# One adaLN transformer block: loads in a new order, idle products first, LN2 normalisation on ScalarE, a new order of instructions

## The chip, the core and the metric

The kernel runs on one core of a Trainium2 chip. Five engines work side by side, each through its own list of instructions, in order: TensorE (PE: matrix products; PEld: its weight loads), VectorE (DVE), ScalarE (ACT), GpSimd (POOL) and SyncE (SP), which issues the transfers (DMAs). Semaphores make one engine wait for another. The metric is the device time of one execution in microseconds (us). "Clock" is the mean granted TensorE clock, 1.00 being full speed. Each run is put down as fast or slow; slow means over 1.5% above the fastest run of the same kernel.

## The reference

An adaLN block on x (2048 x 512, bf16): six modulation vectors from c, sliding local attention with 8 dilated taps and 32 heads, and a SwiGLU FFN with F = 1792.

```python
mod = (_silu(c) @ w_mod).reshape(c.shape[0], 6, 1, -1)
sa, ca, ga, sb, cb, gb = (mod[:, i] for i in range(6))   # shortened
h = _layernorm(x, axis=-1) * (1 + ca) + sa               # LN1
x = x + ga * _A_ref(h, A_wqkv, A_wo)                     # local attention
h = _layernorm(x, axis=-1) * (1 + cb) + sb               # LN2
x = x + gb * _B_ref(h, B_w1, B_w3, B_w2)                 # SwiGLU FFN
```

## The kernel before

The program lists operations with their engine, cost and operands. A list scheduler turns them into one order for each engine, by a table of tuned priorities; semaphores follow from that order. The 2048 rows are 16 tiles T of 128. VectorE takes the statistics, GpSimd turns the variance into 1/sqrt(var + eps) with two 128x1 operations (an add, a power), and VectorE normalises:

```python
def ln_stats(which, T):                       # which: 0 for LN1, 1 for LN2
    i = which * NT + T
    ...
    o = p.op("dve", lambda e: e.bn_stats(st[:, i, :], x_sb[:, T, :]), ...)
    p.op("dve", lambda e: e.bn_aggr(mv[:, i, :], st[:, i, :]), ..., lead=o)
    o = p.op("pool", lambda e: e.tensor_tensor(rs[:, i, :], mv[:, i, 1:2], cst[:, 0:1], ALU.add), ...)
    p.op("pool", lambda e: e.tensor_tensor(rs[:, i, :], rs[:, i, :], cst[:, 1:2], ALU.pow), ..., lead=o)
    p.op("dve", lambda e: e.tensor_scalar(vn.at[:], x_sb[:, T, :], mv[:, i, 0:1], rs[:, i, :],
                                          op0=ALU.subtract, op1=ALU.mult), 350, ("nm", i), ...)
    return vn
```

The result xn is transposed on TensorE, four 128x128 blocks for each tile, and ScalarE applies scale and shift on the way out. The attention multiplies on VectorE: `pq` (128x4096, queries by shifted keys) and `vsh` (128x4096, weights by values), 16 of each, and TensorE sums them with small products. The attention gate is a product against a broadcast copy of silu(c):

```python
def gate(i):
    def mm(e):
        for t in range(KT):
            ins = e.matmul(bank(vm), csb[:, t, :], wm_g[i][:, t, :], start=(t == 0), stop=(t == KT - 1))
    p.op("pe", mm, 4 * MM, ...)
    p.op("act", lambda e: e.activation(dst[:], bank(vm), ACT.Copy), ...)
```

The softmax here doesn't subtract the row's maximum and nothing guards it: scores larger than these inputs give would overflow.

## Time and profile before

| | before |
|---|---|
| time, median of 3 runs | 255.11 us (255.0 to 255.56) |
| profiled span, clock | 253.2 us, 1.00 |
| first projection starts | 10.51 us |
| last VectorE attention product ends | 179.3 us |
| TensorE / VectorE / ScalarE / GpSimd busy | 239.0 / 191.7 / 111.4 / 32.0 us |

A page has the busy time of each engine, then the span in 40 slices, where a digit is a busy share in tenths (9 is 90% or more). A second view lists what an engine waited for: engine, waiting line, releaser, then total us, times and longest. A third, the timeline, gives start, length, engine, line, operation, output from inputs, and how many instructions the row holds.

### The profile page before, as it was taken

How to read it: one execution, taken by the hardware profiler on the slowest of the kernel's cores; microseconds unless marked ns; L12 is line 12 of the kernel's file. 1: busy time of each engine (PE TensorE's matmuls, PEld its weight loads, DVE VectorE, ACT ScalarE, POOL GpSimd, SP SyncE). 2: the span in 40 equal slices, each digit the busy share in tenths (PEclk: the TensorE clock that was granted, in tenths of full speed). 3: DMA queues.
4: the chain of work that ended last, by engine and by line, in shares of the span. 5: the costliest groups of instructions: out<-in, count | busy, mean ns of one | idle time of the engine just before them, and what ended most of it. 6: DMA issues, size and time to landing. Idle time of an engine off the chain costs nothing.

```text
span 253.2 us, 5473 instructions
## 1 busy us (share of the span) xinstructions
PE 239.0 (94%) x2262; PEld 140.4 (55%) x2296; DVE 191.7 (76%) x298; ACT 111.4 (44%) x198; POOL 32.0 (13%) x81
## 2 busy tenths in 40 slices
PE   0599989999999999999999999999999999999995
PEld 0367555655488666546654544556544444565562
DVE  4759889999998989999899899999952443432432
ACT  2159748864863347432462273334234322420120
POOL 6237641001000040000002200020030000000000
PEclk9999999999999999999999999999999999999999
DMA  6997999899954595322369145393001000000101
GB/s 193 359 324 189 293 350 331 210 331 284 241 123 140 142 310 196 64 31 62 106 194 295 54 104 85 87 310 103 4 0 44 0 0 21 21 3 21 41 23 41
DMA packets 45817, 36.29 MB, mean 143 GB/s; under 512 B 19408, under 2 KB 36576, under 8 KB 45792
## 3 DMA queue, kind: packets, MB, share of 16 engines
q1 hardware_dynamic: 45264, 35.94, 49.4%
q8 instruction: 18, 0.29, 0.5%
q10 hardware_dynamic: 528, 0.00, 0.1%
q14 instruction: 7, 0.06, 0.1%
HBM read 30.67 MB, written 5.26 MB: 142 GB/s over the span
## 4 chain that ended last, share of the span: by engine, by line
PE 87%; DVE 5%; DMA 2%; POOL 2%; issue 1%; SPq 0%; ACT 0%; DVEq 0%
PE pall L771 36%; PE pall L792 19%; PE pall L615 9%; PE pall L755 5%; PE pall L742 5%; PE pall L633 5%; PE pall L673 4%; PE pall L574 2%; DMA sb_x<-in_A_x_dram 2%; POOL sb_rs L555 1%; DVE sb_xn L558 1%; DVE sb_st L550 1%; POOL sb_rs L553 1%; DVE sb_pq L664 1%; DVE sb_hh L780 1%
## 5 line engine op out<-in xcount | busy, mean ns | idle before, releaser
L771 PE MATMUL pall<-sb_h,sb_w 128*128 128x512 bf16 (+1 forms) x548 | 100.0, 336 | 0.7
L771 PEld LDWEIGHTS pall<-sb_h,sb_w 128*128 128x128 bf16 x560 | 53.7, 97 | 41.4
L777 ACT ACTIVATE sb_sg<-pall 128x512 bf16<-128x512 f32 (+1 forms) x70 | 35.6, 511 | 70.6 <-PE pall L771 70.3
L780 DVE TENSOR_TENSOR sb_hh<-sb_sg,pall 128x512 bf16<-128x512 bf16 (+1 forms) x70 | 39.5, 577 | 26.0 <-PE pall L771 23.8
L792 PE MATMUL pall<-sb_w,sb_hh 128*128 128x512 bf16 x216 | 49.7, 379 | 0.4
L664 DVE TENSOR_TENSOR sb_pq<-sb_q,sb_kT 128x4096 bf16<-128x4096 bf16 x16 | 36.4, 2283 | 0.5 <-ACT sb_q L622 0.3
L792 PEld LDWEIGHTS pall<-sb_w,sb_hh 128*128 128x128 bf16 x224 | 21.4, 98 | 23.5 <-DVE sb_hh L780 0.2
L615 PE MATMUL pall<-sb_h,sb_wqkv 128*128 128x512 bf16 (+1 forms) x155 | 31.9, 344 | 0.3
L582 ACT ACTIVATE sb_h<-pall,sb_modc 128x512 bf16<-128x512 bf16 (+1 forms) x36 | 23.1, 708 | 18.7 <-PE pall L574 13.1
L553 POOL TENSOR_TENSOR sb_rs<-sb_mv,sb_cst 128x1 f32<-128x1 f32 x32 | 8.8, 276 | 151.4 <-DVE sb_mv L551 148.4
L733 DVE TENSOR_TENSOR sb_vsh<-sb_vsh,sb_al 128x4096 bf16<-128x4096 bf16 x12 | 27.3, 2285 | 0.4 <-DMA sb_vsh<-v_scratch_dram 0.4
L798 DVE TENSOR_TENSOR sb_o<-pall,sb_x 128x512 bf16<-128x512 f32 x16 | 11.0, 688 | 18.0 <-PE pall L792 18.0
L550 DVE BATCH_NORM_STATS2 sb_st<-sb_x 128x6 f32<-128x512 bf16 x32 | 21.8, 682 | 3.3 <-DMA sb_x<-in_A_x_dram 3.2
L555 POOL TENSOR_TENSOR sb_rs<-sb_rs,sb_cst 128x1 f32<-128x1 f32 x32 | 20.9, 654 | 2.5
L615 PEld LDWEIGHTS pall<-sb_h,sb_wqkv 128*128 128x128 bf16 x160 | 15.1, 101 | 11.0 <-ACT sb_h L582 0.7
L633 PE MATMUL pall<-sb_wqkv,sb_h 128*128 128x512 bf16 x63 | 17.6, 411 | 1.5 <-DVE sb_xn L558 1.3
L574 PE MATMUL pall<-sb_ident,sb_xn 128*128 128x128 bf16 x128 | 12.8, 227 | 6.4 <-DVE sb_xn L558 6.4
L673 PEld LDWEIGHTS pall<-sb_E,sb_pq 128*128 128x128 bf16 x512 | 14.7, 96 | 2.7 <-DVE sb_pq L664 0.6
L748 ACT ACTIVATE sb_ot<-pall 128x512 bf16<-128x512 f32 x16 | 9.6, 598 | 13.6 <-PE pall L742 13.6
L574 PEld LDWEIGHTS pall<-sb_ident,sb_xn 128*128 128x128 bf16 x128 | 9.5, 101 | 10.6 <-DVE sb_xn L558 6.9
L755 PE MATMUL pall<-sb_wo,sb_ot 128*128 128x512 bf16 x58 | 15.0, 379 | 0.3
L673 PE MATMUL pall<-sb_E,sb_pq 128*128 128x32 bf16 x512 | 15.1, 177 | 0.0
(59 smaller groups left out, 163.8 us busy)
## 6 DMA issues: line engine op xcount, KB each, us to landing
sb_vsh<-v_scratch_dram SPq DMA_DIRECT2D x48, 256.0 KB, 4.4
sb_vshx<-v_scratch_dram SPq DMA_DIRECT2D x16, 256.0 KB, 4.5
sb_wm_s<-in_w_mod_dram SPq DMA_DIRECT2D x2, 1024.0 KB, 6.6
v_scratch_dram<-sb_v SPq DMA_DIRECT2D x16, 128.0 KB, 5.0
sb_w<-in_B_w_dram SPq DMA_DIRECT2D x4, 512.0 KB, 7.9
out_dram<-sb_o SPq DMA_DIRECT2D x16, 128.0 KB, 1.7
sb_w<-in_B_w_dram SPq DMA_DIRECT2D x1, 1792.0 KB, 8.9
sb_wqkv<-in_A_wqkv_dram SPq DMA_DIRECT2D x3, 512.0 KB, 7.9
```

What stands on the lines that cost most here:

```text
L550: o = p.op("dve", lambda e: e.bn_stats(st[:, i, :], x_sb[:, T, :]), 670, k, r=[vx[T]], w=[vs])
L574: ins = e.transpose(b[:, col:col + P], vns[tt].at[:, ft * P:(ft + 1) * P], ident[:])
L615: ins = e.matmul(bank(vp)[:, 0:n], wqkv[:, t, col:col + P], vh.at[:, t, 0:n], start=(t == 0), stop=(t == KT - 1))
L633: ins = e.matmul(bank(vp), vh.at[:, t, tt * P:(tt + 1) * P], wqkv[:, t, 2 * D:3 * D], start=(t == 0), stop=(t == KT - 1))
L664: return e.tensor_tensor(vp.at[:], in0, in1, ALU.mult)
L673: ins = e.matmul(b[:, c0:c0 + H], vp.at[:, w, ft, :], E_sb[:, ft, :], start=(ft == 0), stop=(ft == KT - 1))
L733: return e.tensor_tensor(v_w, v_w, a_w, ALU.mult)
L755: ins = e.matmul(bank(vy), vt.at[:, ft, :], wo[:, ft, :], start=(ft == 0), stop=(ft == KT - 1))
L771: ins = e.matmul(bank(vp)[:, 0:n], wt[:, t, fi * P:(fi + 1) * P], vh.at[:, t, 0:n], start=(t == 0), stop=(t == KT - 1))
L777: p.op("act", lambda e: e.activation(vt.at[:, 0:n], bank(vgp)[:, 0:n], ACT.Silu), c_act(n), k, r=[vgp], w=[vt], table="silu")
L780: p.op("dve", lambda e: e.tensor_tensor(vh_.at[:, 0:n], vt.at[:, 0:n], bank(vup)[:, 0:n], ALU.mult), c_dve(n), k, r=[vt, vup], w=[vh_])
L792: ins = e.matmul(bank(vz), vhh[fi].at[:, tt * P:(tt + 1) * P], w2[:, fi, :], start=(fi == 0), stop=(fi == NF - 1))
```

## The change

The intent: keep TensorE warm from the start, take small work off it (gates, late transposes), take work off VectorE (the LN2 normalisation), load x of the first four tiles in pairs, and re-tune the order for this new list. All large loads were on SyncE's queue before and still are; what changes is their order, and the scheduler's estimate of when they land. c is now loaded in rows and transposed on TensorE. The core of the diff:

```diff
 def ln_stats(which, T):
     vn = Val("xn", xnpool)
+    if which:
+        vb = Val("nbias")
+        p.op("pool", lambda e: e.tensor_tensor(nb[:, T, :], mv[:, i, 0:1], cst[:, 2:3], ALU.mult), 200, ...)
+        p.op("pool", lambda e: e.tensor_tensor(nb[:, T, :], nb[:, T, :], rs[:, i, :], ALU.mult), 200, ...)
+        p.op("act", lambda e: e.activation(vn.at[:], x_sb[:, T, :], ACT.Identity, bias=nb[:, T, :],
+                                           scale=rs[:, i, :]), c_act(512) + 50, ("nm", i), ...)
+        return vn
     p.op("dve", lambda e: e.tensor_scalar(vn.at[:], ...), 350, ("nm", i), ...)
 ...
 def ln_T(which, gi, vns):
+    if which and gi >= DMA_T:                 # DMA_T = 3: tiles 10 to 15
+        for tt in range(n):
+            p.dma(lambda tt=tt: vh.at[:, :, tt * P:(tt + 1) * P], lambda tt=tt: vns[tt].at[:], ..., transpose=True)
+        ...                                   # scale and shift in place on ScalarE
 ...
+def warm(i, after=()):                        # four idle 128-column products
+    for _ in range(4):
+        ins = e.matmul(bank(vw)[:, 0:P], ones[:], ones[:], start=True, stop=True)
 ...
 def gate(i):
-    ins = e.matmul(bank(vm), csb[:, t, :], wm_g[i][:, t, :], ...)
+    ins = e.matmul(b[:, j:j + 1], wm_g[i][:, t, j * P:(j + 1) * P], csT_bf[:, t:t + 1], ...)
+    ...                                       # transpose, store to memory, load as a broadcast
 ...
+if T >= NT - 2:                               # last two tiles in halves of 256 columns
 ...
-for T in range(4):
-    p.dma(x_sb[:, T, :], x_view[:, T, :], ("load", 1 if T < 2 else 19), 131072, w=[vx[T]])
+p.dma(x_sb[:, 0:2, :], x_view[:, 0:2, :], ("load", 1), 262144, w=vx[0:2])
 ...
-    # table of priorities, all replaced by a new one
```

## The prediction

> **What bounds the kernel now.** I read the page first (busy shares and the 40 slices), then the waits of TensorE, the windows by stage, and the chain of waits with the timeline of the two ends. From the page of the kernel before:
>
> ```profile
> PE 239.0 (94%) x2262; PEld 140.4 (55%) x2296; DVE 191.7 (76%) x298; ACT 111.4 (44%) x198; POOL 32.0 (13%) x81
> ...
> PE   0599989999999999999999999999999999999995
> ...
> DVE  4759889999998989999899899999952443432432
> ...
> PEclk9999999999999999999999999999999999999999
> ```
>
> TensorE (PE) is full in nearly every slice; only the first two or three and the last have room. VectorE (DVE) is nearly as full, but only up to slice 28 (about 177 us). After that it has slack, and PE has not. PE's own waits are short and lie early:
>
> ```profile
> PE pall L574 <- DVE sb_xn L558: 6.4, 2, 5.6
> PE pall L522 <- DMA sb_wm_s<-in_w_mod_dram: 1.5, 1, 1.5
> PE pall L633 <- DVE sb_xn L558: 1.3, 1, 1.3
> PE pall L633 <- ACT sb_q L622: 0.2, 1, 0.2
> ```
>
> The columns are total us, times, longest. 9.4 us of waiting in all, nearly all before the first projection at 10.51 us. A busy share of 94% does not mean full speed, so I look at the spacing of products in the chain of waits (start, length, what):
>
> ```profile
> 10.51 3.59 PE pall L633 x8
> 14.10 0.85 PE pall L615 x4
> 14.95 0.21 PE pall L574 x2
> 15.16 0.85 PE pall L615 x4
> 16.02 0.21 PE pall L574 x2
> ...
> 22.24 0.45 PE pall L574 x8
> ...
> 37.84 0.79 PE pall L673 x32
> ...
> 80.82 3.49 PE pall L771 x32
> ...
> 87.49 0.86 PE pall L755 x4
> ...
> 250.34 0.69 DVE sb_o L798
> ```
>
> Warm rates follow: 0.86/4 = 216 ns for 512 columns, 3.49/32 = 109 ns for 256, 0.45/8 = 56 ns for a transpose, 0.79/32 = 25 ns for the small products. The first rows are slow: 3.59/8 = 449 ns for 512 columns, 0.85/4 = 212 ns for 256. That lasts until about 16 us. The granted-clock row says 9 tenths and more all along, so it does not show this slow start; only the spacing does.
>
> **Adding up the path.** Count of products times warm rate, from the first projection on: q and k 64 x 109 ns + 96 x 216 ns = 27.7 us; v 64 x 216 ns = 13.8; 120 transposes x 56 ns = 6.7; logits and value sums 2 x 512 x 25 ns = 25.3; output projection 13.8; FFN w1/w3 336 x 216 ns + 224 x 109 ns = 96.9; w2 224 x 216 ns = 48.3; second modulation 0.8; the two gates 8 x 216 ns = 1.7. Sum 235.0 us. The kernel takes from 10.51 to 250.3 us, 239.8 us. The difference is 4.8 us: 2.9 us of slow clock (below) and about 1.9 us of small stalls, of which the window from 22 to 40 us alone shows 1.0. Then comes a tail of 2.9 us to 253.2 (an add of 0.69 us, a store). Reported time is 1.9 us above the span (255.11 against 253.2).
>
> **What the Trainium skill says.** (1) "TensorE: Matmul & The Clock Gate", Part 1: the array starts at half clock and is released after about 3.4 us of sustained work. The trace agrees: 449 and 212 ns early, 216 and 109 ns from 16 us. (2) Same page, Part 3 and the gap table: small products cost about 25 ns however few columns. The trace has 25 ns. (3) "ScalarE: Activation LUTs", What ACT_TABLE_LOAD costs: 186 ns + 0.833 ns per column, plus about 93 ns for each per-partition operand, so 0.80 us for 512 columns with scale and bias. The trace's eviction of that form (L582) takes 781 ns. (4) "DMA: Bandwidth & Descriptors", DMA Transpose (X-bar): [...]two transposing streams must not overlap. All six here are on one queue. No run so far shows their duration.
>
> **The change, part by part.**
>
> *Idle products first.* 14 groups of four 128-column products on a tile of ones run from about 1.3 us, with 6 more groups after the first modulation. They fall into idle PE time and leave the array warm. Saved on the path: 8 x (449-216) + 4 x (212-109) x 2 + 4 x (105-56) ns = 1.86 + 0.82 + 0.20 = **2.9 us**. The first modulation (0.99 us cold, 0.78 us warm as at 39.51) is 0.2 us shorter, on the path to the first projection.
>
> *Gates as columns.* Each gate was 4 x 216 = 0.86 us on PE; now 16 one-column products x 25 ns + a small transpose, about 0.5 us. The vector goes to memory and returns as a broadcast, two chained transfers of some 2 to 3 us each (the small store and load of the attention weights take 2.5 us), long before wo is needed. Four VectorE instructions of 250 ns and two ScalarE copies of 0.6 us go. Saved on PE: **0.7 us**; a further 0.4 us if the first gate runs while PE waits for projections.
>
> *Transposes by DMA for T=10 to 15.* 24 x 56 ns = **1.3 us** leave PE. The DMAs are issued after 150 us, where the DMA share is low. They delay only h of the last two groups, while PE has earlier FFN work: hidden.
>
> *LN2 normalisation on ScalarE.* 16 x 0.40 = 6.4 us leave VectorE, 16 x 0.8 = 13 us come to ScalarE (44% busy). Neither is the bound; it only makes stalls rarer.
>
> *Last two tiles in halves.* Same PE time (28 x 109 against 14 x 216 ns), but the last add is of 256 columns (about 0.42 as against 0.69 us) and the last store half as large. Tail: **0.4 us** shorter.
>
> *c in rows.* Tanh waited for c until 3.74 us, while the modulation waited for its weights until 7.73: hidden.
>
> *New order of loads.* By the priorities: x2-3, x0-1, modulation weights, gate weights, x12-15, then v, q, wo, x8-11, k, x4-7. This is the cost. Before the v weights stand 0.52+1.05+0.52+0.52 MB, with them 3.1 MB. The windows show 0.96 MB by 5.6 us, then 365 GB/s to 10.5 (2.75 MB) and 349 GB/s after: 3.1 MB are there at about 11.6 us, as an estimate. Modulation and h would allow a start at about 10.3. The first projection thus slips from 10.5 to about 11.6: **1.1 us lost**, of which the first gate and group 1's eight transposes (0.4 + 0.4 us) fill most. K's weights come only at about 17.5 us, but v and q of T=0 to 3 (7 us) bridge that.
>
> **Sum.** -2.9 -0.7 -1.3 -0.4 +1.1 -0.8 = -5.0 us. For the new order I allow 0.7 us fewer small stalls, mainly those in 22 to 40 us: -5.7 us. 255.1 - 5.7 = **249.4 us**, 2.2% faster.
>
> **Rivals.** (a) *The first stage is bound by DMA.* With late weights the warm array waits instead, and the 2.9 us are lost to waits for wqkv. For it: DMA share 1.04 and 1.10 of 16 engines in 5.6 to 16 us. Against it: PE has other work once v has landed. It would cost up to 3 us: 252.5. (b) *VectorE is the hidden bound* up to 177 us: what PE saves it then waits for pq or attention sums. For it: VectorE is 93 to 98% busy from 40 to 180 us. Against it: it loses 6.4 us itself, and PE has FFN products to fill. About 251.5. (c) *The DMA transposes or the longer normalisation chain come late*, PE waits for h of the last groups, or SyncE's ordered queue holds up the attention loads. Against it: VectorE's attention ends near 177 us, and group [14, 15] is used only from about 220. About 251 to 253. (d) *The new order also removes the remaining stalls* and the first projection does not slip: the counts give 235.0 - 0.7 - 1.3 = 233.0, plus 10.3 start and 2.5 tail = 245.8 span, 247.7 us.
>
> **Range and chances.** The estimate lies almost on the 2% border (250.0 us). (d) sets the low side, (a) to (c) the high: 80% range 247.4 to 252.4 us. I give 0.57 to faster by over 2%, 0.41 to within 2%, and 0.02 to slower, since nothing adds work to PE outside its idle time.
>
> **What the profile after would show.** Products of 128 columns from about 1 us; the first v products 216 ns apart; else step one is wrong. First projection at 10.3 to 11.7 us; a wait of PE for wqkv over 1.5 us proves (a). 104 transposes on L574's successor plus three small ones, and gate products at 25 ns. PE's waits after 20 us under 1.5 us in all; over 3 us, named for VectorE, proves (b), for the transposing DMA or h after 150 us, (c). PE's last product near 245 us, the tail 2.5 us. Wrong would be a sum whose savings are seen yet return as stalls between 20 and 180 us.

## The result, and the profile after

| | before | after |
|---|---|---|
| time, median of 4 runs each, alternating | 255.06 us (254.55 to 255.56) | 268.5 us (264.67 to 270.22) |
| fast runs | all four | 267.99, 264.67 |
| profiled span, clock | 253.2 us, 1.00 | 268.4 us, 0.975 |
| first projection starts | 10.51 us | 15.03 us |
| last VectorE attention product ends | 179.3 us | 200.5 us |

The ratio is 1.0442 [95%: 1.0326, 1.0558]. A ratio here is the mean time of one kernel's fast runs over that of the other's fast runs of the same rounds, so it is not quite the ratio of the quoted medians. Where I turn a ratio into microseconds, I multiply its excess over 1 by 255.1: the changed kernel costs 11.3 us. Its profiled run is a slow one, at 270.22 us, but all four of its runs have a clock of 0.968 to 0.975, so the clock is no mark of the slow runs alone. The mean clocks of the two kernels are not quite comparable: that of the kernel before reads 1.00 from the start, although its first products are 449 ns apart (see the prediction), so its slow start is not in its mean.

The page of the changed kernel, same lines as those shown of before, with GpSimd's row added:

```profile
PE 246.7 (92%) x2376; PEld 149.2 (56%) x2407; DVE 187.0 (70%) x283; ACT 123.8 (46%) x214; POOL 54.1 (20%) x113
...
PE   7598999798579979699999999999999999999996
...
DVE  5568989799296896689999989882795344162342
...
POOL 5245122004240044600000450400462100000000
PEclk9889999999798999979999999999999999999999
```

TensorE has holes in slices 9 to 16 (counted from 0), some 60 to 114 us, where before it was full. GpSimd's busy time rose from 32.0 to 54.1 us for 32 more 128x1 operations. It is busy where TensorE has these holes, and again in slices 22 to 30, where TensorE stays full. TensorE's waits:

```profile
PE pall L629 <- ACT sb_xn L596: 9.1, 4, 3.4
PE pall L533 <- DMA sb_wm_s<-in_w_mod_dram: 2.5, 1, 2.5
```

The largest by far is for the normalised xn, from ScalarE. And ScalarE itself had waited for GpSimd:

```profile
ACT sb_xn L596 <- POOL sb_nb L595: 23.6, 11, 6.0
```

The timeline shows why. First the kernel before, one LN2 tile:

```profile
61.99 0.18 DVE L551 BATCH_NORM_AGGREGATE sb_mv<-sb_st 128x2 f32<-128x6 f32 x1
...
62.25 0.19 POOL L553 TENSOR_TENSOR sb_rs<-sb_mv,sb_cst 128x1 f32<-128x1 f32 x1 [21.04 <-DVE sb_mv L551]
...
62.52 0.55 POOL L555 TENSOR_TENSOR sb_rs<-sb_rs,sb_cst 128x1 f32<-128x1 f32 x1
...
62.88 0.39 DVE L703 TENSOR_TENSOR sb_tr<-sb_ex 128x256 f32<-128x256 f32 x1
...
65.09 0.73 DVE L558 TENSOR_SCALAR sb_xn<-sb_x,sb_mv,sb_rs 128x512 bf16<-128x512 bf16 x2
...
66.44 0.61 PE L574 MATMUL pall<-sb_ident,sb_xn 128*128 128x128 bf16 x8
```

The add takes 0.19 us and the power 0.55. Beside them VectorE runs short operations of the next tile and of the softmax. When it comes to the normalisation, rstd has long been there. Now the changed kernel, the first LN2 tile:

```profile
63.55 0.18 DVE L585 BATCH_NORM_AGGREGATE sb_mv<-sb_st 128x2 f32<-128x6 f32 x1
63.65 4.46 DVE L719 TENSOR_TENSOR sb_pq<-sb_q,sb_kT 128x4096 bf16<-128x4096 bf16 x2
...
63.81 2.14 POOL L587 TENSOR_TENSOR sb_rs<-sb_mv,sb_cst 128x1 f32<-128x1 f32 x1 [19.44 <-DVE sb_mv L585]
...
66.03 2.48 POOL L589 TENSOR_TENSOR sb_rs<-sb_rs,sb_cst 128x1 f32<-128x1 f32 x1
...
68.49 0.18 POOL L594 TENSOR_TENSOR sb_nb<-sb_mv,sb_cst 128x1 f32<-128x1 f32 x1
68.75 0.19 POOL L595 TENSOR_TENSOR sb_nb<-sb_nb,sb_rs 128x1 f32<-128x1 f32 x1
68.97 0.81 ACT L596 ACTIVATE sb_xn<-sb_x,sb_nb,sb_rs 128x512 bf16<-128x512 bf16 x1 [3.51 <-POOL sb_nb L595]
...
69.84 0.61 PE L629 MATMUL pall<-sb_ident,sb_xn 128*128 128x128 bf16 x4 [3.43 <-ACT sb_xn L596]
```

VectorE no longer normalises, so nothing keeps the scheduler from placing two `pq` products straight behind the statistics. They run from 63.65 to 68.11. The 0.19 us add takes 2.14 us and ends with the first product; the 0.55 us power takes 2.48 and ends 0.4 us after the second. The chain that took 0.8 us takes 5.1, and TensorE, whose transposes stand next in its order, waits 3.43 us. The profile has 11 GpSimd operations longer than 1.5 us after the change: one in LN1 and ten in LN2. Before it had two of that length and one of 1.42 us, all in LN1.

The Trainium skill states this case, on a page that the prediction did not use: "SBUF — State Buffer", Who interferes with whom. A VectorE instruction with both inputs in SBUF contends with a GpSimd instruction that reads SBUF, since they share a read interface, and the one that comes second waits until the first is done. The trace agrees: 2.14 and 2.48 us against 0.19 and 0.55, ending with the products.

The windows by stage say how much it costs (us from:to and length, busy us of PE, PEld, DVE, ACT and POOL, then clock, DMA share, GB/s). The changed kernel:

```profile
60.00:80.00 20.00, 14.45 (x251) 9.46 (x251) 15.07 (x20) 8.28 (x15) 8.22 (x8) 0.91 0.74 205
80.00:100.00 20.00, 19.24 (x249) 14.50 (x247) 16.40 (x21) 9.95 (x21) 3.20 (x4) 0.92 0.78 209
100.00:120.00 20.00, 16.64 (x175) 9.95 (x179) 14.29 (x18) 11.33 (x17) 6.97 (x13) 0.91 0.34 89
```

TensorE stands idle for 9.7 us here (5.55, 0.76 and 3.36), nearly all of it in four waits for xn of 3.43, 1.78, 1.56 and 2.29 us; in the kernel before it was 0.5 us in the same windows, at clock 1.00. The clock fell as well: 2 us slices show 0.50 in 70 to 72, in 80 to 82 and in 114 to 116 us, right behind the waits of 3.43, 1.78 and 2.29 us. A mean of 0.91 over 20 us means 3.6 us at half speed, which is 1.8 us of work lost; over the three windows 5.2 us. Together 14.9 us. This is a slow run, which lost 15.2 us of span in all. As a check the products done by a given time were counted by their weight loads, each product at its warm duration. The changed kernel is 3.3 us behind at 60 us (43.5 against 46.8 us of work) and 16.8 behind at 120 (90.0 against 106.8): 13.5 us are lost in those 60 us. From there to 180 us no more is lost, though GpSimd stands still four more times: by then TensorE has FFN products to go on with.

### The profile page after: what moved, and what is told of

It is laid out like the page before. It is cut to its first block, busy times and chain, and to the rows that moved or that the text cites. A ratio compares the mean times of both kernels' runs of the same rounds, so it can differ in the third digit from the quotient of the medians.

```text
span 268.4 us, 5746 instructions
## 1 busy us (share of the span) xinstructions
PE 246.7 (92%) x2376; PEld 149.2 (56%) x2407; DVE 187.0 (70%) x283; ACT 123.8 (46%) x214; POOL 54.1 (20%) x113
## 4 chain that ended last, share of the span: by engine, by line
PE 65%; DVE 11%; DMA 8%; POOL 7%; SPq 4%; issue 2%; ACT 2%; DVEq 0%
PE pall L826 35%; PE pall L862 14%; PE pall L810 4%; SPq L133 4%; DMA sb_wqkv<-in_A_wqkv_dram 4%; PE pall L797 4%; DVE sb_pq L719 3%; POOL sb_rs L587 3%; POOL sb_rs L589 3%; PE pall L728 2%; PE pall L849 2%; DMA a_scratch_dram<-sb_attn 2%; POOL sb_nb L594 2%; DMA sb_al<-a_scratch_dram 2%; DVE sb_w L895 1%
## 5 line engine op out<-in xcount | busy, mean ns | idle before, releaser
L587 POOL TENSOR_TENSOR sb_rs<-sb_mv,sb_cst 128x1 f32<-128x1 f32 x32 | 18.5, 577 | 149.9 <-DVE sb_mv L585 144.1
L862 PE MATMUL pall<-sb_w,sb_hh 128*128 128x512 bf16 x189 | 45.1, 386 | 0.4
L670 PE MATMUL pall<-sb_h,sb_wqkv 128*128 128x512 bf16 (+1 forms) x155 | 29.4, 335 | 1.4 <-DMA sb_wqkv<-in_A_wqkv_dram 1.1
L862 PEld LDWEIGHTS pall<-sb_w,sb_hh 128*128 128x128 bf16 x196 | 18.8, 98 | 20.9 <-issue 0.8
L788 DVE TENSOR_TENSOR sb_vsh<-sb_vsh,sb_al 128x4096 bf16<-128x4096 bf16 x11 | 25.0, 2284 | 2.3 <-DMA sb_al<-a_scratch_dram 1.9
L872 DVE TENSOR_TENSOR sb_o<-pall,sb_x 128x512 bf16<-128x512 f32 (+1 forms) x18 | 11.2, 629 | 19.8 <-PE pall L862 14.7
L637 ACT ACTIVATE sb_h<-pall,sb_modc 128x512 bf16<-128x512 bf16 (+1 forms) x30 | 19.2, 708 | 11.1 <-PE pall L629 11.1
L596 ACT ACTIVATE sb_xn<-sb_x,sb_nb,sb_rs 128x512 bf16<-128x512 bf16 x16 | 12.8, 810 | 23.6 <-POOL sb_nb L595 23.6
L629 PE MATMUL pall<-sb_ident,sb_xn 128*128 128x128 bf16 x104 | 10.7, 232 | 9.7 <-ACT sb_xn L596 9.1
L814 DVE TENSOR_TENSOR sb_x<-pall,sb_x 128x512 bf16<-128x512 f32 x16 | 11.0, 686 | 10.2 <-PE pall L810 9.9
```

What stands on the lines that cost most here:

```text
L670: ins = e.matmul(bank(vp)[:, 0:n], wqkv[:, t, col:col + P], vh.at[:, t, 0:n], start=(t == 0), stop=(t == KT - 1))
L788: return e.tensor_tensor(v_w, v_w, a_w, ALU.mult)
L862: ins = e.matmul(bank(vz), vhh[fi].at[:, tt * P:(tt + 1) * P], w2[:, fi, :], start=(fi == 0), stop=(fi == NF - 1))
```

## The experiments

Sixteen kernels ran. "Order kept" means that the list of operations was edited after the scheduler had done its work, so that each engine's order of all other instructions stays. Without that, any edit of an operation reorders everything, as the first run shows. A is the theory that the GpSimd chain standing still under VectorE products is the cause. The rivals: the new order by itself, the DMA transposes, the late loads, the idle products.

### Does the chain on GpSimd cause it?

**Normalisation back on VectorE, scheduler free.** `if which:` became `if False:`.

> One part of the change undone: the LN2 normalisation is back on VectorE (x minus mean, times rstd, one instruction of 0.4 us), so the two extra GpSimd instructions per tile and the ScalarE instruction go; the list scheduler orders the rest anew, with the priorities of the changed kernel. Theory A (the GpSimd instructions of the second layer norm sit behind VectorE's 2.2 us products on bf16 operands, because with the norm off VectorE the scheduler puts such a product right after the statistics): VectorE now has to wait for rstd itself, small work lies beside GpSimd, TensorE's waits for xn between 60 and 120 us fall from 9.1 us to under 3 us, and the time from 268 to 252 to 258 us. Rival B (the new order of products and loads as such): still above 262 us.

Measured: 280.4 us, ratio 1.0961. That is slower still, and by the ranges it would count for rival B. But the order changed wholesale: TensorE now waited 6.2 us for `pq` and 5.4 for `vsh`. So this run decides nothing between the two; it shows that the priorities are tuned to one exact list of operations.

**The chain taken from GpSimd, order kept.** The four GpSimd operations of each LN2 tile became two short VectorE ones straight behind the statistics. The power is left out, so rstd is wrong.

```diff
-add, pow, mult, mult on "pool"
+rs = mv[:, 1:2] + EPS                 on "dve"
+nb = (mv[:, 0:1] * -1.0) * rs         on "dve"
```

> A wrong result on purpose. The order of TensorE, ScalarE and SyncE is that of the changed kernel, instruction for instruction; only the four GpSimd instructions per tile of the second layer norm are gone, and two small VectorE instructions right behind the statistics take their place (var+eps without the power[...]; and the bias). Theory A: no GpSimd instruction is left in that chain to be held up, so TensorE's waits for xn from ScalarE fall from 9.1 us to under 2 us, the granted clock in 60 to 120 us returns to 1.0, and the time falls from 268 to 250 to 256 us, though VectorE gets 6 us more work. Rival B (TensorE's order asks for LN2's transposes too early, whatever engine makes rstd): waits for xn stay above 6 us and the time above 262 us.

Measured: 258.35 us (256.01 to 262.19), ratio 1.0095 [1.0023, 1.0167], clock 0.987. TensorE waits for xn from ScalarE nowhere; from 60 to 120 us it is busy for 59.6 of 60 us at clock 1.00. Order of TensorE, ScalarE and SyncE is the changed kernel's, so neither that order nor the ScalarE normalisation costs these 1.0442 - 1.0095 = 0.0347, or 8.9 us. They go with the GpSimd chain.

**A guard in a correct kernel, first form.** The chain goes right behind the statistics in the list, and the very next VectorE operation waits for it if it is longer than 1 us.

> The changed kernel with its order kept on every engine, and a correct result. One thing is added: where a VectorE instruction of over 1 us follows the statistics of the second layer norm, it waits until the four GpSimd instructions of that tile are done. Theory A (GpSimd is held up by the big VectorE products): no GpSimd instruction of the second layer norm lasts over 1.5 us any more, TensorE's waits for xn from ScalarE fall from 9.1 us to under 3 us, and the time from 268 to 257 to 262 us although VectorE now waits about 1.3 us in some ten places. If the port is not the cause, the added waits can only cost: 268 to 280 us.

Measured: 265.82 us, ratio 1.0414 [1.0369, 1.0458]. Five LN2 operations stood still all the same, since in many places the big product was the second or third operation. TensorE still waited 6.1 us for xn. The time is 3.8 us above the range of A. It is half a guard, but it fits: half the stalls left, two thirds of the waits left.

**The guard widened** to the first long one among the next four VectorE operations. All values are right.

```diff
+for aggr, chain in self.chains:                  # after scheduling, before the semaphores
+    ...                                          # chain moved right behind aggr
+    nxt = [o for o in self.placed[at + 4:] if o.eng == "dve"][:4]
+    big = next((o for o in nxt if o.cost >= 1000), None)
+    if big is not None:
+        big.deps[chain[-1]] = True
```

> The run with the guard mended: in the changed kernel, orders kept and result correct, the first VectorE instruction of over 1 us among the four that follow the statistics of a tile of the second layer norm waits until that tile's four GpSimd instructions are done (the first guard looked only at the very next one, and five held-up instructions stayed). Theory A: no GpSimd instruction of the second layer norm over 1.5 us, TensorE's waits for xn from ScalarE under 3 us, granted clock in 60 to 120 us back above 0.97, time 255 to 261 us. If the port is not the cause: 264 to 275 us.

Measured: 260.53 us (259.02 to 263.91), ratio 1.0192 [1.0153, 1.0232]. The same tile, in the timeline:

```profile
62.29 0.19 POOL L605 TENSOR_TENSOR sb_rs<-sb_mv,sb_cst 128x1 f32<-128x1 f32 x1 [18.12 <-DVE sb_mv L603]
62.55 0.55 POOL L607 TENSOR_TENSOR sb_rs<-sb_rs,sb_cst 128x1 f32<-128x1 f32 x1
```

The chain is short again in all 16 tiles, TensorE's waits for xn are gone, and VectorE pays 8.8 us of waiting in eight places. One sign was missed: the clock from 60 to 80 us is still 0.91 (then 1.00). Net gain 1.0442 - 1.0192 = 0.025, or 6.4 us. A holds in a correct kernel too.

**The normalisation alone in the kernel before**, order kept: ScalarE normalises, two more GpSimd operations for each LN2 tile, VectorE's instruction gone.

> The kernel before with one part of the change alone: the second layer norm's normalisation on ScalarE with a bias made by two more GpSimd instructions, in the places where VectorE did it; all orders kept. Theory A' (the part does harm only together with an order that puts a big VectorE product beside the chain, and in the order of before small VectorE instructions lie there): at most two GpSimd instructions of that chain over 1.5 us, time 253.5 to 258 us. Rival (ScalarE and the longer chain are harmful in themselves): over 260 us.

Measured: 257.46 us, ratio 1.0103 [1.0071, 1.0134], or 2.6 us lost. The short operations behind the statistics protect the first half of the chain here, but two of the added multiplications met a product:

```profile
170.44 2.23 POOL L583 TENSOR_TENSOR sb_nb<-sb_mv,sb_cst 128x1 f32<-128x1 f32 x1
```

So the move is no gain by itself in the old order either, and most of its cost in the changed kernel needs the new order, which puts products right behind the statistics.

**The normalisation alone undone in the changed kernel**, order kept: VectorE normalises right behind the statistics.

> The changed kernel with the one suspected part undone and the order kept on every engine: the LN2 normalisation is again one VectorE instruction, right behind the statistics (or behind the statistics that follow them), so that VectorE waits for rstd itself; the two further GpSimd operations and the 16 ScalarE ones are gone. Theory A (the normalisation on ScalarE lets a 2.3 us VectorE product start behind the statistics, and the GpSimd chain stands still under it): like the kernel with guards, 257 to 261 us, no GpSimd operation of LN2 longer than 1.5 us, TensorE waits no longer for xn. Rival (the part is harmless, the new order is the cause): 264 to 268, as the changed kernel.

Measured: 269.44 us, ratio 1.0538 [1.0475, 1.0602]: a miss for A, which had said 257 to 261. GpSimd never stands still in LN2 and TensorE no longer waits for LN2's xn. But what VectorE waits for says where the time went:

```profile
DVE sb_xn L623 <- POOL sb_rs L614: 14.9, 16, 0.9
```

and TensorE in turn:

```profile
PE pall L889 <- DVE sb_hh L862: 2.1, 2, 1.2
PE pall L824 <- DVE sb_vsh L815: 1.6, 2, 0.9
```

Sixteen waits of 0.93 us and 6.6 us of work are 21.5 us of VectorE's time, against 8.8 with the guards. TensorE then waits for VectorE in several places. The kernel before pays one such wait in LN2 (0.71 us, at 187 us); in the tile shown above, its order puts short work between statistics and normalisation. So A must be put more narrowly: the fault is not that ScalarE normalises, for in this order VectorE doing it straight behind the statistics costs as much. The fault is that long products meet the chain on GpSimd.

### The rival causes

**All transposes on TensorE** (`DMA_T = 5`).

> One part undone: all transposes of the second layer norm on TensorE, none by DMA. Theory A says the loss lies in 60 to 120 us, where no DMA transpose runs: the time stays within 3 us of the changed kernel's 268 us (24 transposes of 56 ns, 1.3 us, come back to TensorE). Rival C (the DMA transposes hold up SyncE's queue or come late): falls below 262 us.

Measured: 272.8 us, ratio 1.0664, 1.8 us above the range of A, and TensorE waits for xn from ScalarE 9.2 us as in the changed kernel. Its profiled run is a fast one and has the same ten stalls in LN2. The DMA transposes are not the cause. (The order shifted a little, so the extra 5 us are not their worth.)

**The old priorities with the new parts.** If the new order were the whole cause, the old one should cure it.

> One part undone: the priorities, and with them the order of loads and products, are those of the kernel before; all other parts of the change stay. Theory A: the four GpSimd instructions and the big VectorE products still meet, since the scheduler knows nothing of it: GpSimd instructions over 1.5 us in LN2's chain still show, TensorE still waits for xn, and the time is 258 to 268 us. Rival B (the new order is the cause): 248 to 254 us, since the savings on TensorE now show.

Measured: 291.93 us, ratio 1.1424. Worse by far, and outside both ranges:

```profile
PE pall L728 <- DVE sb_pq L719: 6.4, 5, 2.0
PE pall L629 <- ACT sb_xn L596: 4.9, 2, 3.9
```

The rival in this form fell. Old priorities on a new list are not the old order, though, so this does not say what the new order is worth.

### Where the predicted savings went

**The idle products alone in the kernel before**, order kept: 14 groups of four from the start, four groups after the first modulation.

> The kernel before with one part of the change alone: 14 groups of four idle products from the start and 4 groups behind the first modulation, all orders kept. By the step of the prediction (2.9 us of slow clock from 10.5 to 16 us plus 0.2 us of the modulation): the first v products are 216 ns apart instead of 449, and the time falls from 255.1 to 252 us (251 to 253.5). Rival: VectorE, ScalarE or the loads bind in 10 to 25 us, and the time stays at 254 to 255.5 us.

Measured: 255.12 us, ratio 1.0003 [0.9965, 1.0042]: nothing gained. The warm start is real. In its timeline:

```profile
10.86 1.67 PE L661 MATMUL pall<-sb_wqkv,sb_h 128*128 128x512 bf16 x7 [0.90 <-DVE sb_xn L586]
...
37.70 0.29 PE L602 MATMUL pall<-sb_ident,sb_xn 128*128 128x128 bf16 x2 [0.82 <-DVE sb_xn L586]
```

and the kernel before:

```profile
37.56 0.29 PE L574 MATMUL pall<-sb_ident,sb_xn 128*128 128x128 bf16 x2 [0.75 <-DVE sb_xn L558]
```

The v products are 216 ns apart instead of 449. But the first starts 0.35 us later than in the kernel before, and TensorE now waits for weights, which it did not before:

```profile
PE pall L643 <- DMA sb_wqkv<-in_A_wqkv_dram: 1.5, 2, 1.0
```

So of the 2.9 us only about 1.0 is left at 22 us, by the same count of products; at 30 us it is 0.4, at 40 and 50 us none. The transposes at 37.6 us wait for VectorE's xn in both kernels, and VectorE was not made faster: in the chain of waits of the kernel before, VectorE and GpSimd alternate from 24.7 us up to that point.

**The same with guards**, to see whether the GpSimd stalls of LN1 hold that chain.

> The kernel before, order kept, with the idle products (255.1 by themselves) and with the guard for LN1 and LN2: no VectorE product longer than 1 us starts before the GpSimd pair of the tile's statistics is done. If the three GpSimd stalls of LN1 (22.8, 27.4 and 34.3 us, 6.3 us in all) hold the chain of VectorE and GpSimd that absorbed the warm start's 2.9 us: the transposes at 37.6 us come 1 to 2 us earlier and the time is 252.5 to 254. If VectorE's own work holds that chain: 254.8 to 255.5.

Measured: 256.3 us, ratio 1.0043 [1.0003, 1.0084]. A miss for the stalls: no GpSimd operation over 1 us is left, and nothing is gained. The time is above the other range too (254.8 to 255.5). That VectorE's own work holds the chain, and that the guard's waits only add to it, is the reading that remains, not shown by itself.

**Transposes by DMA and the last tile in halves, in the kernel before**, order kept, five rounds.

> The kernel before, orders kept, with the two parts of the change that lie after VectorE's stage: the last tile in two halves of 256 columns, and the transposes of tiles 10 to 15 by DMA. By the prediction's steps, 24 x 56 ns = 1.3 us and 0.4 us: 255.1 to 253.4 us (252.8 to 254.2). Rival: the DMA's latency of 2.4 us holds up ScalarE, which takes the place of the saving: 254.5 to 257 us.

Measured: 255.47 us, ratio 1.0011 [0.9987, 1.0036], not the 1.7 us of the prediction. ScalarE waits for the transposes, and TensorE for ScalarE and VectorE:

```profile
ACT sb_h L661 <- DMA sb_h<-sb_xn: 7.1, 2, 5.9
```

```profile
PE pall L814 <- DVE sb_vsh L805: 1.4, 1, 1.4
...
PE pall L843 <- ACT sb_h L661: 0.9, 1, 0.9
```

The tail did shrink, from 2.9 us to 2.5 behind TensorE's last product. What was spared came back as 2.3 us of waits, at 174.7 and 193.5 us; for the first of them VectorE itself had waited 1.7 us for a load of `vsh` (0.4 us in the kernel before) that was on its way while the first two transposes were issued. That they delayed it is not shown.

**How dear is VectorE, how dear TensorE?** Twelve further statistics (8.2 us) on VectorE, or 40 further 512-column products (8.6 us) on TensorE, in the kernel before.

> The kernel before, orders kept, with VectorE given 12 more statistics instructions of 0.68 us (8.2 us in all), whose results nobody reads, at tiles 0 to 11 of the second layer norm. If VectorE is a bound of its own up to 177 us (what the idle products alone suggested, 2.9 us saved on TensorE and nothing gained): 260 to 264 us. If TensorE alone is the bound, as the prediction had it: 255 to 257.5 us.

> The kernel before, orders kept, with TensorE given the output projection of tiles 0 to 9 twice (40 products of 216 ns, 8.6 us in all, same result). If TensorE's time counts wherever it falls, as the prediction's sum had it: 262.5 to 264.5 us. If VectorE alone sets the pace up to 177 us: 255 to 259 us.

Measured: 257.24 us (ratio 1.0086, +2.2 us) and 263.85 us (1.0341, +8.7). TensorE is the bound: added work costs its whole length. VectorE has slack, but not much: a quarter of what is added shows up.

### What is left over the kernel before

The guarded kernel still loses 4.9 us (1.0192). Three runs looked for them.

**The order of loads on the kernel without the GpSimd chain**: v's weights before the gate's, wo last.

> The kernel without GpSimd in the second layer norm's chain (the run of 258 us, wrong in value on purpose), with the order of its first loads changed and nothing else: x, modulation weights, v weights, gate weights, x of tiles 12-15, q weights, k weights, the other x, zeros, and wo last, where wo had stood before the k weights. Theory D (what is left over the kernel before, about 6 us of useful products missing by 60 us, comes from late weights in the first 25 us): the first projection starts by 12.5 us instead of 15.1, waits for wqkv vanish, and the time falls from 258 to 250 to 254 us. Rival: if the loads are hidden, it stays at 256 to 260 us.

Measured: 258.21 us, ratio 1.014 [1.0078, 1.0202], against 1.0095 without the new order of loads. First projection at 16.58 us; a miss. The gate product stands ahead of the v products in TensorE's order, so earlier v weights could not help.

**The order of loads on the guarded kernel**: x of the first tiles, modulation weights, gate weights, v.

> The changed kernel with guards (260.5), orders kept on the four computing engines, only the order of loads on SyncE changed: x0-1 and the first modulation weights first, gate weights, v, x12-15, q, k, the other x, wo last. If the late weights are what is left of the loss over the kernel before: first projection before 13 us instead of 15 and 257 to 258.5 us. If what the early projections gain is absorbed later, as it was when the kernel before was given a warm start: 260 to 261 us.

Measured: 262.04 us, ratio 1.0191 [1.0139, 1.0243]: no gain. The edit missed its aim. The 1 MB of modulation weights now ran beside x of tiles 0 and 1, whose statistics started at 7.46 us instead of 3.67, and since silu(c) stands behind them in VectorE's order, the first projection came at 16.46 us. Whether late loads cost something thus stays open.

**The guarded kernel without idle products.**

> The changed kernel with guards (260.5), order kept, all 80 idle products taken out. If they win what the prediction said (2.9 us): 263 us or more. If their gain is absorbed behind the projections, as in the kernel before: 260 to 261.5. If they themselves hold TensorE (they stand in its order ahead of the first projections): below 260.

Measured: 258.88 us (258.24 to 263.83), ratio 1.0138 [1.0098, 1.0178], against 1.0192 [1.0153, 1.0232] with them. They win nothing. The time is in the range of the third case (they hold TensorE), but whether they cost something is not settled, for the intervals overlap.

Both of the last kernels have runs near 259 to 260 us and runs near 264. The profiled ones fell in the slow state, and the windows of the reordered loads show what is slow there:

```profile
64.00:66.00 2.00, 0.00 (x0) 0.00 (x0) 2.00 (x1) 0.15 (x1) 0.00 (x0) 0.82 0.66 184
...
70.00:72.00 2.00, 2.00 (x60) 1.83 (x57) 2.00 (x2) 0.83 (x2) 0.00 (x0) 0.50 1.03 355
```

TensorE waited 3.03 us for a `pq` product up to 66.16 us; the clock then stands at 0.50 to 74 us. The mean of 0.74 over 60 to 80 us is 5.2 us of work lost, by the rule above. I have no profile of a fast run of these two, so that the half clock makes the difference is not shown.

No run beat the kernel before.

## Why the prediction was wrong

**"LN2 normalisation on ScalarE ... Neither is the bound; it only makes stalls rarer."** This is the step that failed. It priced the move by the busy times of VectorE and ScalarE, 6.4 us off the one and 13 us onto the other; ScalarE's 0.81 us for one is as said. It left out the GpSimd chain in between, which the change doubles from two operations to four, and what VectorE would do in the freed place. Before, the operations behind the statistics were short. After, they were products of 2.28 us, and the chain stood still under them. Measured: 8.9 us with the chain taken away, 6.4 net in a correct kernel with guards. The chances named only 0.02 for slower, "since nothing adds work to PE outside its idle time"; but waits need no added work.

**"Idle products first ... 2.9 us."** Alone in the kernel before, the warm rates came as said; the gain on the path was 0 (1.0003). The step took time saved before 16 us for time saved at the end. Rival (a), waits for weights, took 1.5 us of it at once; rival (b), VectorE as a hidden bound, took what was left: the transposes at 37.6 us stand where VectorE puts them. In the changed kernel the array did not even stay warm: the clock is 0.50 from 12 to 14 us, after the 2.5 us wait for the modulation weights and in spite of the idle products, and it is back only at the first projection.

**Transposes by DMA, 1.3 us, and the tail, 0.4 us.** The transposes left TensorE and the tail got 0.4 us shorter; the sum on the time was 0.3 us the wrong way, within the interval of none. Rival (c) described it: ScalarE waited 7.1 us for the transposes.

**The slip of the first projection, 1.1 us lost.** It slipped by 4.5 us, to 15.03. The modulation weights landed at about 9.87 us and not at 7.76, and the transfers ran at 66 and 182 GB/s in the fifth and sixth microsecond, where they had run at 369 and 360 before. The estimate had taken over the old rates. That is 2.1 of the 4.5 us. The rest lies between the first modulation and the first projection, and there too a load came last: without the idle products (run a7_no_warm) TensorE waited 1.79 us for the v weights and began at 14.91 us. Why the loads were slow is open.

**Fewer small stalls, 0.7 us, gates, 0.7, filling, 0.8.** No run measured them alone. Without the GpSimd chain's stalls the changed kernel is at 1.0095, some 257.5 us, while the prediction's sum with all six savings struck out is 255.1 + 1.1 = 256.2. But in that run the first projection comes at 15.15 us, 4.6 us late and not 1.1, and VectorE is busy for 190.4 us, 3.4 more than in the changed kernel. So how much of these savings reached the end cannot be read from it; what did was less than what was lost.

**What held:** TensorE is the bound (8.6 us added cost 8.7). And the last sentence of the prediction, that wrong would be savings that return as stalls between 20 and 180 us, is what the trace shows, by way of an engine that it had not looked at.

**Open:** what the 2.4 us beyond the chain are (the late first projection is the first candidate, not tested), and what the new order is worth by itself.

## What to carry to other kernels

When an operation moves to another engine, write down the whole chain of engines between its inputs and its users, with the idle ones too, and ask what the freed engine will run in that place. A 0.19 us operation on GpSimd can last as long as the VectorE product beside it. On an engine that runs in order, keep short operations, or a wait, behind whatever starts such a chain. Time saved early counts only if the next meeting with another engine moves as well: before adding up savings, look for the next wait behind each.

## What the Trainium skill lacked or had wrong

- "GPSIMD Engine Reference", 1. Specifications, names the contention with VectorE without saying what it does to a small operation. The full rule is on "SBUF — State Buffer", Who interferes with whom. The runs put numbers to it: 128x1 operations of 0.19 and 0.55 us took 2.14 and 2.48 us under 2.28 us products. Nothing in either page had to be corrected.
- "TensorE: Matmul & The Clock Gate", Part 1, ties the fall to half clock to about 3.4 us of idling. That agrees with the 3.43 us wait of the changed kernel, and roughly with 3.03 us in another run. But two of the three falls between 60 and 120 us in the changed kernel came right behind waits of 1.78 and 2.29 us, while a wait of 1.56 us had none behind it. In the guarded kernel the clock fell to 0.50 at 67 to 69 us although the longest wait just before was 0.80 us; in the 3.5 us before the fall lay mostly products of 1, 16 and 32 columns. The page speaks of frequent micro-idling for another kernel, but not of how short waits and such small products count. No run isolated it.
- "DMA: Bandwidth & Descriptors", DMA Transpose (X-bar), gives no duration for a small transpose within SBUF (elsewhere the page has a bandwidth). The six of 128x512 bf16 took 2.4 us from issue to landing (median) in the changed kernel, 2.7 in the kernel with only these parts.
